# Gate logits gathered by expert in one PSUM bank, and no GpSimd in the last region of a fused attention and two-MoE kernel

## The chip, the cores and the metric

The kernel runs on one core of a Trainium2 chip. The metric is device time in microseconds of one execution of the whole program. The core has TensorE (matmuls; its weight loads are shown apart, as PEld), VectorE (DVE), ScalarE (ACT), GpSimd (POOL) and SyncE (SP), which here issues all loads and stores. [...]

## The reference, cut to what matters

```python
def reference(**kw):
    x = attn(**kw)                        # (4, 8, 768, 48) -> 3072 tokens x 384
    x = soft_moe(x, phi, w1, w2)          # 8 experts x 4 slots
    return top1_moe(x, w_gate, w1, w2)    # 8 experts

def attn(q, k, v, a_re, a_im):            # per batch and head, state S complex, 48 x 48
    for t in range(768):
        S = a[t][:, None] * S + outer(k[t], v[t])     # a scaled so that |a| <= 0.999
        y[t] = q[t] @ S.real

def soft_moe(x, phi, w1, w2):
    logits = x @ phi                                  # 3072 x 32
    d = softmax(logits, axis=0)
    slot_in = (d.T @ x).reshape(8, 4, 384)
    slot_out = concat(relu(slot_in[e] @ w1[e]) @ w2[e] for e in range(8))   # 32 x 384
    return softmax(logits, axis=1) @ slot_out

def top1_moe(x, w_gate, w1, w2):
    logits = x @ w_gate                               # 3072 x 8
    p = softmax(logits, axis=1)
    e = argmax(logits, axis=1)
    return p[e] * (relu(x @ w1[e]) @ w2[e])           # token by token
```

All arrays are 32-bit floats. w1 is 8 x 384 x 1024 and w2 is 8 x 1024 x 384, in each of the two MoE layers.

## The kernel before, in words

The 3072 tokens are 24 units `u` of 128 tokens (4 batches of 6 chunks). The program has three regions, and in each the work is first declared and then issued by a planner.

**Region 1** is the attention in chunks, the phi logits and the column softmax with its running sums. Its matmuls are small (48 to 128 rows and columns). Products of q, k and v with decay factors (the tiles F, line 573) are made on VectorE or GpSimd, and a part of F is copied by DMA into another layout (M, line 578). The first loads of soft-MoE weights ("late weight pieces", line 425) run here as soon as their buffers come free.

**Region 2** (lines 866 to 1117, declared in part by `decl_row`, `decl_dev` and `decl_c4`) is the soft-MoE: w1 and w2 of all eight experts over the 32 slots (L918, L947, L982), which gives the slot outputs so4 (L988). Beside it run the row softmax of all tokens, and its weights cc, which are split into high and low halves in c4. Since the softmax weights are close to uniform, the index `ei` of the second MoE's expert is found early, from the mean slot output, and the loads of that expert's weights (m1, m2) use it as a register.

**Region 3** (lines 1122 to 1307) is the second MoE. The transposes of L1054 turn c4 into cS, [96 features, 3072 tokens], copied out of PSUM six times (512 columns each). The gate weights for the slots, so4 times w_gate, are made at L1079 and split into W2S. The gate logits are 24 matmuls, one per unit: 128 tokens of cS against the 8 columns of W2S (L1089), all into one bank; the gate chain follows on VectorE (max, equality, exp, sum, reciprocal).

The two layers of the chosen expert are not computed token by token, since all tokens lie near the mean slot output. For 1024 hidden units, Gs = so4 times m1 (L1173, two halves of 512), is turned (L1180: G) and squared (ACT, L1177; L1181), and each hidden unit is sorted into "on for all tokens" (`pos`, L1184 to L1188), "off for all" or "mixed" (`mixed`, L1187), of which at most 96 are handled. The running counts of the mixed ones (L1193 to L1197) give `pf` (L1200), from which the selection matrix Pm is made by comparing with iota (L1202, two instructions, one per half). `Gp` (L1206) is G masked with `pos`; `PmF` (L1210, L1211) is the plain-float copy for the last two of the eight weight blocks. `Gl` (L1201) is G's low half. m2 is split into m2h (L1143) and m2l (L1145), in three pieces of two blocks. Then W, the matrix by which all tokens are multiplied, is summed in one PSUM bank `kb_a` by L1225 (plain), L1233, L1237 (m2h) and L1241 (m2l), and copied out as W0 (ACT, L1251) and W1 (DVE, L1252). The output stage has six groups of 512 tokens: one 512-column matmul for the hidden values (L1260), their relu and its low half (ACT or DVE L1261/L1262, DVE L1264), then for each of four units three 384-column matmuls (L1270, L1271, L1274), a copy out scaled by the gate (L1282 or L1283, ACT or DVE) and a store (SP).

**What sets the order.** An operation is declared with an engine, a modelled duration, what it reads and writes, and the other engines that could do it. `follow` (line 211) reads a string, ORDER[k], one 16-bit number per operation: operation number times four plus which alternative of engine. The order of the numbers is the order of issue, so every engine's queue follows from the string. `place` (line 148) then simulates it to hand out PSUM banks, and `emit` (line 223) issues it; where TensorE would be idle in that simulation, `emit` puts in dummy matmuls (line 844). The trace shows none of these in region 3. [...]

After the last region the program checks on the device that the shortcut held and branches to a full computation otherwise (line 1478 is in it); it is not taken here.

Of the kernel before, what the change touches and what calls it, by code (L numbers as in the profile page):

```python
# [44 lines left out]
def feature_rows():  # L45
# [24 lines left out]
    "8~`W)3;-Yi7yv8)6aX{;H~=sJ1OPn%KmY&$Q~<O9xBw6UXaHmY2mmAiL;y$tYyeCEyZ}%DZ~(yor~#A!bpV(EcmTx!kN}(jqyTvWYyofq<^Z4otN^e8d;ov|0Rqebr~p6#i~z_0)Bw={kO5o(_yFtx"  # L70
    "eFBsLm;s#ugaAYV$N`7|NCEu;p#h`;bOB5OtN{T5^#IHP`~Xn_@BnxL&;hUkd;wGev;l+xfC1b9xB*xJ)B))L7y;M--2sUKTmiuW!~y661OW&E3;`4Y*#YDM-~hY<904o=XaP6_5CQB0AOSoB-~sIc"
    "i~;EZ@Bw84U;$(Sa0BoHBmpP^Gy!M=fCBUa90CLa2m%cPFah}j6ax?f90M5wAOk=H`~oln6as_-C<9aji2_6eBm*o1FarPs1Or$DNdt5PGy?Pi_yLRpl>(3g7y}>zBmyV`m;#&vTmz{CGy@0&cmr$#"
    "Z~~wL5Cbd%OapWROaeFpJOV%hr2~8egac#)Py(z1r~+vN#01C$fCJzHqyh{BFb0eRECxgZv;w#SU;}Ielmom1hy#%Wm;=B9%mhUQNCH^`!~&cHumaEmL<L9%RRZt?Oa;&cNdzDT)dCO&6$Q8hyaUw)"
    "7zI!S*aRE}tOGO#wFCGB`~+MA!2<vV$O6m)umfQNPzA&T$O8xkOaxc}%mdT|&;!5(+yvkR4FymGp#vxdECo0QYy><8*aO@H3<LxPFa<aTGzH`Ycm(VO-~;3X=mYEnR0Z?{=mdNO_ybe~fCPvH@B@4X"
    "JOy0@U<9-Vbp!zfgam*FSp+}^lmwUr`~%nmTm@tWSOsAPga(`hpaf(DX$0f~R0g>P5D0Jti3ULhL<YPCqy&rvkOYkexCZnDaRo>QyavDq6bRG>-38bMumm^(Bn21<v;<%V;01UE=>>cRJppJ1WCo}N"
    "tOVr+Yz2S?hy_>%Yz7<%APATS#06*uU<gbG1O#;k#0G=~WC(Bu5CohCkOrg%j0I2zkOg!Flm!U{$Oh~M@CCpH$pxSWXb5Zw&<1!0^aWf7m<1FB%m%atC<dqo7zEt{BnYhroCTx>00smG*ap=G_yx=b"
    "6b6_Gkq2=IL<sx^@CKj-I0QHdJOmsBxCHbDoCu8v{00OE0SEa8d<ZB6ECjp>C<w3yv<J8e(FLdn90#BX2nM|blm@T`AO|c6Km-g1u?MUNy$9_E5C%vH=>|9lqzJeNJP1$-9R@H2Ob9RtR0!Y(Gz3`)"
    "p$7;D3<ul>7zX49bO<yEzy}Zq#0L}yzzHM=7zcm|hzL9fln12;m<PxQ&<7+0%m+{hTnh*YC<nv|+y~$X$O)_nAOu(ogb1hzkO(XXj0nsL<OeVZT?pt0)CaT(ya?<EKnU0eun4&b;0ZYiGzUQk_y=GM"
    "{RcP-MF#{5)CiOa-3Z_a><K&y<p@*>Kni3F@CVokJqhUu3<zKe00<lk2ns|B@CoDz_zBPns0#!L^a-2?XbaQ{Yzqtutqa5m00{&MSPAq8{0UtNR0rq@APVdVzzFaN^avCRC<<^3X$g1;BnkiuWC?T&"
    "fCp>|a0v(r5DGvEFbc>BL<w{W%?S7iGzlCDAPM{k*a^@GEDC%Hv<XNGObSp6+zAW`5D7F2Q3-$vhzX1d6bTp!SO;7OU<Y^!O$i7Mgb7s&kO?FSC<&AaWCvIZ<qDVyNCyNBO$TTPgbN@BNeLwej0<22"  # L80
    "=n8NLunV*cga@1nTncmti3fNK><Xv_pb4l6;0vt<kPDOx3=0(txC^BT<O^mB01M~~p$qH_5DN$km<yZ>#0z{2X$ou#a0(a;bP9Y5cnS;+@Cu|01Pg!)919=|5DgR!$P2s+gbFAN%nR5H^a>;k+zZqT"
    "hzigP7z!*4^b7q8_zUq1`U?CD7!9Zj=njkukP74ulnMb1fD0@QhzlGI1Pm|>KnpYrI14-rNee{_cn81>Fb!-6R1KI4SPe7{g$!H`><$bJFb{kOI1LC4ED0G56bz&aC=4(O91LI$j13?Rs0=L(febMW"
    "B@AQ@a19_0j0~9!JPkw*kqwj$hzytwKn+L@@D5B3oD4_|l?<Q^XbnsZuneUPtO~6RGz>Tlv<&<VBn@N?R12I9G!LK+d<>`!JPbe#xC~GXL<|rNXbi9lybM$f&<t1%U;x+(zzp;b)C@QeTnu0gYz_Dh"
    "qz%Xn#SO#^*bFEQ+zj9h3=d2Y%nWo5cnxt3Yz)B-v<kQiQ4R16><q9C)D5i-+zNmVObfgUcn<syoC<sm$O_F0Q42f|P!NO-;0h2AC=O%~We%YV-3_=6<P59{u?ZLt$PFA1(G4IENDtTzX%3tav<*}c"
    "SP*~?Xb)@;eGZHchz-pRC=c`vi4KqqgbpkZ01x;L=?o+faSxyn5DwrC<PDGxm=0_XybW*;l@9z3=nd=*To3>b01faBoDQH41P=%gKo4{eq!6SIC=#p=Ob-MO6b=**s19Hd2o6vWcn^UOd=G>VT@Q2+"
    "bq=%+xDLDys1OVe7!E`aSP#Gs#11SHunuGp&<d>(bPRb6R1e(`co2~f9S(pH(GJuQ)eeXc$PU;Jgb;`jxDWsk*$<2ll@OQ^)C!Cc-45*!*$`k4%?<<*^bC9ukPyTQ^bh?H2@v@Yun?FJoDY=`tPk7}"
    ";12Q+pbw}Iq!0KE<PWe9yb$0J=@2Xq;13`WzzWb0Xb`jy3=p^vz!1$4Fb?bx^$^Gq5D*j)7!WiLBoO5g@DRKY5E1zh01?CxJPsfZB@X-$v=AH+=?^pztq~Lvun|ZOOb!_l!4K3AP!b#wAQ8n6B@uKI"
    "FcK&bI1bPdJP|Y!ED$gdKoMCEc@jhsd=do_I1o4zJP-^KffBS4Y!Gk|C=o0XND(j*I1yY9$PqjeU=Ga@g%Ye1u@ck~*b!I~ToN=9h!P4Bv=WdKOc78K+!47F;1O66T@ld{^btT3z!6{)Y!XxvxDk{R"
    "WD-CQa1xjjr4q#vpb|t9WD!Ub!4mip<PrQ4yb|aUNDyce>=9rQ#1a4!yb;I}bP;e7@DX?s=o0J_OcJ0GP!0qV2oekuL=K!1d=Z2Z92FcA5E392R1(+{XcTP}@Ddagj1p`UkP%c47!s)xNE96t2ovBE"
    "_!9IIf)i;IbQ5qBq!E4-KoFD>kP~nebrdKS3=>5VP!tgp7!y<!OcYoY$PZi;fDvdBgcCFqI1`Bzj1z4U)Di*{loKEmBooXJsSy<toD(z^1QVGPC=)CbcoTROP!l{8pcAAMFcUx%L=&hJtP}haR1?e+"  # L90
    "xD!Ydyc56^<Pu;Mh!K1gj1hnouoHz8OcRI{#1qgG+!DwW)e~G3v=i79m=VkqoDo<P<P+!<>=W=4_!AHmloX5<oD`rGkQ6u-nH2OBq!g?a&=ar}v=pcmAQBuDAQS);B@+A-1QfUwycA^=z!cmQ$P^?L"
    "C=|sMU=!37;1gsMEEF&l*c1p9Bo#Ci+!W*#6cjuZ3=}XG5EVca%oO+(I27O%@Dvyn6crd1(G=(u{S@>REEPl)>=XzU3>5$s1Qh",
    "FaU@E000aD5CIec7y%psKmY^)2mlNK5C9YaAORQvGypgNMF2<uJOE7q8~`8yBmgJ?EC7rEd;lZ?C;==1Fab0HI029VoB){sJOMxfZ~$}wO#x8>Q~`JZL;*+vl>l4;PynC+WC3geSplQ~U;tnNr~p*}"
    "SO9bZWdK|NXaH>htN^e8gaCj5X#unVxB$cey#T-f$N<a$@BsJ#`~Uy}&;Zl`*Z|}J2mu5E-2mVK=m2p6c>(MI^Z)",
    ")ByMb&;Z;3%m9!8@B+vHC;%(~*Z=?km;e|65C9|rlmHw6ECDb8^a3aWGyyOH6aY8@-~d1YL;*Aar~o(s<NyQ!=>SLptN;iAJOJ<j_yGL?3;-Yi00Ha(^Z-Br1OW^IL;ySiv;dp{xBwIZOaZX~2mwd{"
    "Q~_N95CI(lPyr+Wpa8@GhyhFhSOJUyPyl2BVF4HcAOXMtbOBTVTmWbRSO9zhgaLp6gaEt%hyaWLkO5!-WB_acXaH;hZ~>$NsR5J$tO29|cmaR`m;syt`~m<2=mG2j1Oo^I90DK$umQ*cpaHZ2yaBlZ"
    "zya_96aypz)B)K690SY&Fak9KC;|)uPy$r~!~xs^-~rJAEdme%SONqB2?FE+NCNx;^Z@_@gaY{iKmv#YI06^~JpvR0MFLC$TmoSNi~?i=xB{30Xaal!oC1&nl>)E=Yyxxwr~+{Uy#l}jZ~$}wcmkjT"
# [1468 lines left out]
```

## Time and profile before

| | |
|---|---|
| Median of 3 runs | 293.49 us (292.86 to 293.55) |
| Profiled execution: its own time | 295.17 us |
| Profiled execution: span | 293.4 us, mean granted TensorE clock 0.96 |
| Busy, share of the span | TensorE 259.0 us (88%), weight loads 215.1 (73%), VectorE 222.4 (76%), ACT 208.5 (71%), GpSimd 85.3 (29%) |
| Moved by DMA | 65.41 MB, mean 223 GB/s |
| Region 1 / 2 / 3 end at about | 217 / 249 / 293 us of the span |

The profile is one execution recorded on the chip. Times are microseconds from the start of its span; the execution's own time is longer than the span, by what lies around it, and the median of the runs is another set of executions. A row of the chain of waits is a step of the work that ended last, followed backwards: its start, its length, the engine, the tile and the line. "issue" in it is time in which the engine waited for nothing that the profile shows. A timeline row is one instruction, or several alike in sequence; [x <- y] behind it is how long its engine had been idle and what ended that. The timeline's durations of matmuls are modelled ends and overlap each other, so the chain's lengths are used for sums.

### The profile page before, as it was taken

The numbers are of one execution on the slowest core, as the hardware profiler recorded it, in microseconds if no ns is written. First come the engines' busy times: TensorE is split into PE (matmuls) and PEld (weight loads), VectorE is DVE, ScalarE is ACT, GpSimd is POOL, SyncE is SP. The second block draws the span as 40 slices with busy tenths as digits, with TensorE's granted clock in tenths as the row PEclk, the third lists the DMA queues.
The fourth block names the chain that finished last, engine by engine and source line by source line (L and its number), as shares of the span: only waits on it lengthen the run. The fifth ranks groups of instructions, "written<-read, shape, count | busy, mean of one in ns | idle before, by whom it ended". The sixth has DMA issues, their size and how long they took to land.

```text
span 293.4 us, 11835 instructions
## 1 busy us (share of the span) xinstructions
PE 259.0 (88%) x4959; PEld 215.1 (73%) x4959; DVE 222.4 (76%) x489; ACT 208.5 (71%) x448; POOL 85.3 (29%) x128
## 2 busy tenths in 40 slices
...
GB/s 215 271 172 113 171 240 259 326 256 284 255 228 292 242 193 256 255 177 266 269 190 223 256 133 275 209 211 192 269 349 280 373 127 234 200 1 0 261 305 91
DMA packets 31789, 65.41 MB, mean 223 GB/s; under 512 B 3584, under 2 KB 16256, under 8 KB 31728
## 3 DMA queue, kind: packets, MB, share of 16 engines
...
## 4 chain that ended last, share of the span: by engine, by line
PE 62%; DMA 11%; DVE 10%; ACT 8%; issue 4%; POOL 0%; SPq 0%; DVEq 0%; POOLq 0%; ACTq 0%
PE bank L627 9%; PE bank L518 9%; PE bank L683 8%; PE bank L668 7%; DMA wr<-w 5%; PE bank L649 4%; PE bank L604 3%; DMA M<-F 3%; PE bank L947 3%; PE bank L716 3%; DMA kqi<-kq 2%; ACT L847 2%; DVE F L573 2%; PE bank L918 2%; PE bank L1270 1%
## 5 line engine op out<-in xcount | busy, mean ns | idle before, releaser
L627 PE MATMUL bank<-F 48*64 48x128 f32 (+1 forms) x1152 | 39.8, 247 | 1.1 <-DVE kqi L527 1.1
L627 PEld LDWEIGHTS bank<-F 48*64 48x64 f32 x1152 | 36.1, 133 | 3.7 <-DVE kqi L527 1.3
L847 ACT ACT_TABLE_LOAD x29 | 37.2, 1283 | 1.2 <-PEq L1549 0.8
L683 PE MATMUL bank<-sc,v 128*64 128x64 f32 x768 | 33.2, 234 | 1.8 <-POOL v L588 1.6
L683 PEld LDWEIGHTS bank<-sc,v 128*64 128x64 f32 x768 | 27.7, 145 | 7.5 <-issue 4.2
L668 PE MATMUL bank<-F,St 48*64 48x128 f32 x480 | 27.2, 278 | 4.3 <-issue 3.4
L518 PE MATMUL bank<-cst,wl 128*128 128x128 f32 x192 | 26.8, 281 | 2.4 <-ACT wl L490 2.4
L637 DVE TENSOR_TENSOR sc<-bank,cst 128x384 f32<-128x384 f32 x48 | 25.4, 549 | 3.5 <-PE bank L627 3.4
L518 PEld LDWEIGHTS bank<-cst,wl 128*128 128x128 f32 x192 | 23.5, 191 | 4.0 <-ACT wl L490 2.8
L668 PEld LDWEIGHTS bank<-F,St 48*64 48x64 f32 x480 | 18.8, 133 | 6.8 <-issue 4.9
L588 POOL COPY v<-v 64x192 f32<-64x192 f32 x31 | 14.0, 452 | 30.8 <-DVE F L573 11.1
L627 PE MATMUL bank<-M 48*64 48x64 f32 (+1 forms) x384 | 21.8, 245 | 1.2 <-DMA M<-F 1.2
L448 ACT COPY kT<-bank 128x96 f32<-128x96 f32 (+1 forms) x66 | 19.7, 355 | 4.2 <-PE bank L604 3.3
L649 PE MATMUL bank<-v,kT 128*48 128x48 f32 x640 | 21.4, 212 | 1.3 <-issue 1.3
L573 DVE TENSOR_TENSOR F<-kqi,wl 128x768 f32<-128x768 f32 x24 | 22.2, 957 | 0.4 <-ACT wl L553 0.2
L627 PEld LDWEIGHTS bank<-M 48*64 48x64 f32 x384 | 19.1, 134 | 2.3 <-DMA M<-F 1.4
L649 PEld LDWEIGHTS bank<-v,kT 128*48 128x48 f32 x640 | 17.9, 126 | 3.9 <-issue 2.9
L604 PE MATMUL bank<-cst,F 128*128 128x128 f32 x120 | 19.3, 284 | 0.2
L541 POOL TENSOR_TENSOR wl<-wl,n 128x384 f32<-128x384 f32 x12 | 12.1, 1006 | 23.9 <-DVE n L540 6.4
L448 ACT COPY yT<-bank 112x256 f32<-112x256 f32 x29 | 10.3, 374 | 12.0 <-PE bank L683 11.9
L573 POOL TENSOR_TENSOR F<-kqi,wl 128x768 f32<-128x768 f32 x8 | 14.7, 1833 | 11.3 <-PE bank L518 6.1
L668 PE MATMUL bank<-M,St 48*64 48x128 f32 x160 | 13.3, 286 | 2.3 <-issue 2.3
...
## 6 DMA issues: line engine op xcount, KB each, us to landing
...
v<-v SPq DMA_DIRECT2D x24, 288.0 KB, 4.2
...
```

The source lines that it names most:

```text
L448: v = {"A": ("ACT", t_act(n, True), lambda: nc.scalar.copy(out=out, in_=in_()), False), "D": ("DVE", t_dve(n), lambda: vec.tensor_copy(out ...
L518: pe.matmul(bank(kb)[:, 128 * i:128 * i + 128], lt[:, j, 128 * i:128 * i + 128], (tri, tri2)[j], start=True, stop=True)
L541: either("P", 384, lambda e: e.tensor_tensor(out=lt[:, 1], in0=lt[:, 1], in1=n, op=ALU.subtract), r=[kth, kn], w=[kth])
L573: either(e, 768, lambda e, i=i, b=b: e.tensor_tensor(out=Fv[:, i], in0=kq, in1=b, op=ALU.mult), r=[(kkq, 0), (kkq, 1), klt(u, i)], w=[kF[i]])
L588: alt=(("POOL", 350, lambda src=src, dst=dst: pool.tensor_copy(out=dst, in_=src), True), ("DVE", t_dve(192, True), lambda src=src, dst=dst ...
L604: pe.transpose(bank(kb)[:, 128 * j:128 * j + 128], F[:, j, 128 * x:128 * x + 128], idn)
L627: pe.matmul(o, kind(2 * m + y, i, x)[:, t:t + 64], kind(2 * m + y, i, 2 + x)[:, t:], start=(x == 0), stop=(x == 1))
L637: op("DVE", t_dve(384), lambda i=i, msk=msk: vec.tensor_tensor(out=sct[scs[i]], in0=bank(kbs[i])[:, :384].rearrange("p (m t) -> p m t", m= ...
L649: pe.matmul(kvps[64 * i:64 * i + 48, q, 48 * x:48 * x + 48], w, v[:, 48 * h:48 * h + 48], start=True, stop=True)
L668: pe.matmul(out(q, i, 64), S[64 * i:64 * i + 48, o:o + 64], kind(q, i, 2 + x), start=(x == 0), stop=False)
L683: pe.matmul(out(q, i, 64, 64 * b, 64), v[:, h:h + 64], sct[scs[i]][:, m, t:t + 64], start=(c == 0), stop=(c == 0 or b == 1))
L847: tab = lambda t: nc.scalar.preload_act_table_set(TABLES[t])
```

## The change

Four things change in the code; the cut diff shows them.

1. The column of the gate for unit u is `gx(u)` instead of u, in the scaling of the outputs and in the full computation.
2. W2S has 88 columns instead of 8. A new VectorE operation in region 2 fills them with zeros; the gate weights are written in columns 40 to 47. The logits are six matmuls, one per group of 512 tokens, with W2S as the weights (48 columns of it, in a window that moves by eight per group, so that group m's eight experts land in rows 8m to 8m + 7 of one bank) and 512 columns of cS moving. All six accumulate in the same bank. ACT (or VectorE) copies the [48, 512] result into `hid[0]`, and four transposes turn it into the bank from which the gate chain reads as before.
3. m2h, m2l and `Gp` lose their GpSimd alternative.
4. The three ORDER strings are new.

```diff
+def gx(u):
+    return 6 * (u % 4) + u // 4
...
-    W2S = t2("W2S", [128, NE], F32R)
+    W2S = t2("W2S", [128, 88], F32R)
+    V(88, lambda: vec.tensor_scalar(out=W2S, in0=tri[:, :88], scalar1=0.0, scalar2=None, op0=ALU.mult), [], ["W2Z"], True)
...
-        split(kb_g, W2S, NE, "W2S")
-        kb_l = s.bank()
+        split(kb_g, W2S[:, 40:48], NE, "W2S")
+        kb_t, kb_l, L = s.bank(), s.bank(), hid[0]
         for m in range(6):
-            def f(m=m):
-                for u in range(4 * m, 4 * m + 4):
-                    pe.matmul(bank(kb_l)[:, NE * u:NE * u + NE], cS[:96, 128 * u:128 * u + 128], W2S[:96], start=True, stop=True)
-            M(540, f, ["W2S", ("cS", m)] + ([kb_l] if m else []), [kb_l] + ([] if m else ["lg"]), None if m else kb_l)
+            M(250, lambda m=m: pe.matmul(bank(kb_t)[:48], W2S[:96, 40 - 8 * m:88 - 8 * m], cS[:96, 512 * m:512 * m + 512], start=(m == 0), stop=(m == 5)),
+              ["W2S", ("cS", m)] + ([kb_t] if m else []), [kb_t], None if m else kb_t)
+        AD("A", 512, lambda: nc.scalar.copy(out=L[:48], in_=bank(kb_t)[:48]), lambda: vec.tensor_copy(out=L[:48], in_=bank(kb_t)[:48]), [kb_t], ["lgT"])
+        def f():
+            for b in range(4):
+                pe.transpose(bank(kb_l)[:, 48 * b:48 * b + 48], L[:48, 128 * b:128 * b + 128], idn[:48, :48])
+        M(400, f, ["lgT"], [kb_l, "lg"], kb_l)
...
-           alt=(("DVE", ... m2h ...), ("POOL", ... m2h ...)))
-        either("D" if k % 2 else "P", n, ... m2l ...)
+           alt=(("DVE", ... m2h ...),))
+        either("D", n, both=False, ... m2l ...)
...
-        either("D", 64 * ns, ... Gp ...)
+        either("D", 64 * ns, both=False, ... Gp ...)
...
-            g1 = gate[:, u:u + 1]
+            g1 = gate[:, gx(u):gx(u) + 1]
```

What the new strings hold, decoded:

- Region 1 (1359 operations, the same ones): TensorE has 368 and SP 165 operations before and after; VectorE goes from 385 to 391, GpSimd from 114 to 109, ACT from 327 to 326; ACT table loads stay 29. Of the F products (L573) seven go from VectorE to GpSimd and four the other way. The load of w_gate goes from the 105th to the 121st of SP's operations. Of the late weight pieces, ten instead of five are issued ahead of unit 22's M copies (L578), and none instead of four after those of unit 23.
- Region 2: TensorE's order is the same. VectorE has the new zeros as its second operation, three of the six casts of c4 (one before) and one difference more than before. The six late loads of w2 change places among themselves.
- Region 3, GpSimd: three m2l and two Gp before, nothing after. All five go to VectorE.
- Region 3, VectorE after, from so4 on: small constants and zeros, cS of group 0, hc0 pf0 G0 mixed0, m2h piece 0, pf0 hc1 pf1 mixed1, Gl0 Pm0 Gl1 pos0 pos1 Gp0 pf1 Gp1 Pm1, m2l0, GpF, m2l1, m2l2, then the gate chain, W1 and the copies of the output stage.
- Region 3, TensorE after: gate weights, cS 5 0 1, Gs0, logits 0, cS2, sq0 G0, Gs1, cS4, counts 0, G1 sq1, cS3, logits 1, the zeroing of kb_a, logits 2, counts 1, logits 3, Gm0, logits 4, hi1, logits 5, lo0 hi2 Gm1 lo1, the four transposes, h0, ml1 A3 ml2 lo2 ml0 hi0 A4, then the output stage. (Gm is L1215; h0 the first L1260; lo and hi are L1233 and L1237, ml L1241, A L1225.) Before: cS 5 0 3 2, Gs1, gate weights, sq1 G1, the zeroing, Gs0, cS1, logits 0, G0, cS4, and so on.
- Region 3, SP: m1 in halves 0, 1 (before 1, 0), m2 in pieces 0 1 2 3 4 (before 1 2 0 4 3). The last store is 384 KB (before 192 KB). Of the 24 scaled copies of the outputs ACT has 14 and VectorE 10 (before 17 and 7).

## Rows read from the trace of the kernel before

**Rows 1.** Busy time by stretch: us, engines (instructions), granted clock, DMA share, GB/s.

```profile
core 0: us, PE busy (x) PEld busy (x) DVE busy (x) ACT busy (x) POOL busy (x), PEclk, DMA share, GB/s
230.00:240.00 10.00, 9.44 (x95) 3.74 (x94) 2.11 (x5) 3.70 (x10) 1.75 (x4) 1.00 0.77 268
...
256.00:257.00 1.00, 1.00 (x19) 1.00 (x18) 0.54 (x5) 0.83 (x2) 0.44 (x2) 1.00 0.00 0
257.00:264.00 7.00, 5.10 (x27) 4.97 (x26) 6.64 (x12) 0.36 (x1) 4.39 (x3) 0.55 0.00 1
...
271.00:282.00 11.00, 11.00 (x62) 10.40 (x62) 6.71 (x14) 9.10 (x17) 0.00 (x0) 1.00 0.72 267
```

**Rows 2.** The chain of waits: start, length, what.

```profile
135.73 2.28 issue
...
193.92 3.84 DMA M<-F
...
225.78 13.40 DMA wr<-w
...
248.06 0.57 DVE so L988
...
253.65 1.49 DVE pos L1188
...
258.07 1.66 DVE PmF L1210
259.73 2.09 DVE Pm L1202
...
268.25 0.35 PE bank L1241 x2
...
268.94 0.65 PE bank L1225 x2
```

**Rows 3.** Timelines of GpSimd, VectorE, TensorE and ACT, 251 to 262 us.

```profile
253.31 1.81 POOL L1145 TENSOR_TENSOR m2l<-wl,m2h 128x768 fp32r<-128x768 f32 x1 [20.49 <-PE bank L1173]
...
257.49 3.90 POOL L1145 TENSOR_TENSOR m2l<-wl,m2h 128x768 fp32r<-128x768 f32 x2
...
256.06 0.15 DVE L1188 SCALAR_TENSOR_TENSOR pos<-pos,mixed 128x4 f32<-128x4 f32 x1
...
257.13 0.81 DVE L1202 TENSOR_TENSOR Pm<-cst,pf 128x384 fp32r<-128x384 f32 x1
...
261.86 0.87 PE L1215 MATMUL bank<-Pm,G 128*96 128x96 f32 x4 [1.90 <-DVE Pm L1202]
...
251.04 0.28 ACT L1177 ACTIVATE sq<-bank 128x128 f32<-128x128 f32 x1 [0.68 <-PE bank L1173]
```

**Rows 4.** Groups of VectorE instructions by line and shape: busy, mean ns.

```profile
L573 DVE TENSOR_TENSOR F<-kqi,wl 128x768 f32<-128x768 f32 x24 | 22.2, 957 | 0.4 <-ACT wl L553 0.2 <-PE bank L668 0.2
...
L541 DVE TENSOR_TENSOR wl<-wl,n 128x384 f32<-128x384 f32 x4 | 2.2, 550 | 0.0
L1262 DVE TENSOR_SCALAR hh<-bank 128x512 fp32r<-128x512 f32 x3 | 2.1, 692 | 3.7 <-PE bank L1260 3.7
```

**Rows 5.** The chain of waits again, for TensorE's groups.

```profile
248.67 1.51 PE bank L1054 x12
...
250.19 0.79 PE bank L1173 x24
...
250.98 0.77 PE bank L1079 x6
...
251.96 0.33 PE bank L1180 x2
...
256.24 0.45 PE bank L1089 x4
...
274.45 0.23 PE bank L1260
```

**Rows 6.** Timeline of SyncE's queue, 200 to 222 us.

```profile
203.62 16.80 SPq L425 DMA_DIRECT2D wl<-w  x28
```

**Rows 7.** Waits: engine, line, waited for; us in total, times, longest.

```profile
PEld bank L683 <- issue: 4.2, 22, 0.4
```

More of the change, by code (lines that the diff above doesn't have):

```diff
@@ L69 @@
 ORDER = [
[L70 to L97, printed above, removed]
@@ new lines @@
+    ";1S>w<Pqo*1QA^kBo$>5OcGQQz!JR@C>3oI*%4q71{25<@DltH020I!>=ASkp%L&A&=QCe*b-0<R1WwNloEIm1QG}m3=*6Ym=dKD5EASX2oq2ga1tC6q!Dlt92KAvj1m|Uyb&N3sS>CWL=Jorgb@rA"
+    "5ff+;Y!ht}6cZg2X%pNM6cQN|0uyKyNEB@p$PdjAa1?YDgcFbxKoCR_fDw=pG!s-5SQLE|I1`x@loNpy_!5*6AQM~^oD<9v^b-9Nc@%sUP!s49BoinTJQHvebQ5_KR1+){pc60?j1hnoh!dm}OcX2?"
+    "I2EiDKodk0xD!Ydyc5(CmJ~1*h!Ln0U=)lKg%pSsuoL7GOcS&d%oETPz!St1G!@7b)f1QzoDo<PToc$6<P+!<Wfbfa@Dq#__!IOKoD{GWkQAU4q!gJHv=kr`tP}tg92BS&xD>n;z!W7C5ER4|AQZ?H"
+    "+!NswBortVEEF&lG!!@#U=w8%)D#312o(Gi*c3bz+!W*#6cj)d3=|O+%oO+(859&1;1uu_L=^oL7!}bJ>=XzU^b`yg02SyI1Qh",
@@ new lines @@
+    "hyVZpFaQhz5CIec1ONyC7y%psKmZ^CGypgN3;-knMF2<u5C9YaC;=D%8~`8yECDb9GyyySI01|RJOMxfL;+0zkN}wgQ2`_XC;%(~Spif5NCA`pOaWX0U;$|XZ2^1$PynC+qyU@%U;wB9Z~=7zcmaI@"
+    "Z~#>RfB<*^SO8@JTmWbQZ2)utumFSrv;epO!~nejzyQbq%mAza@BsJ#`~Uy}1OW&E&;Zl`WdYa#<N)0O-~i|V>;Uut",
+    "`~m<2_yU*!&;T$1<NzoD007hgGyn(yoB%igEC37upa9$e-~iYF>;Uut1px2>JOB^?qyYQ?_y80D009UAECDb9umB(c1p&MO3<0SCGyx<46ag3kH~~NbJOM}nOaUAL7yv*3=m10jL;+L*AORczTmeV`"
+    "C;?0W5CO;lPyr+Xv;c?!Pyko~zyNpwWC36SlmT!7tN>I1gaK>;bOE>kSO91N!~k3XWB_0QtO2kAi~+O(hyZ8+i~x`T%m8cvbO4+Im;sOhfB}2~paG--1Oo^IZ~*WDBm$@b^Z^V55Ca?oxB<igyaAK|"
@@ L99 @@
+    "!2!?#_yNcP)B)T9%>mc}<N+uGECT2O3<3}W6aoYS-~sFb`~esO2m&Ai00JBWi~^7XKmtetL;{ooOad?hGy+rtI0C=|m;yZlodQq-paP@<xB^%LTmq;9umZFK#RA9z)B@N7+ydbOtOCpecmQAmd;k;!"
+    "yaHqbXadm!@B-ul=>lv5a02WCBm?vUfB=L5d;)+1bOLz-gaU{H7y}>!C<6",
 ]
@@ L1143, in build @@
         op("ACT", t_act(n), lambda h=h: nc.scalar.copy(out=m2h[:, h], in_=m2[:, h]), r=[("m2", k)], w=[("m2h", k)], tab="E",
-           alt=(("DVE", t_dve(n, True), lambda h=h: vec.tensor_copy(out=m2h[:, h], in_=m2[:, h]), True), ("POOL", t_pool(n), lambda h=h: pool.tensor_copy(out=m2h[:, h], in_=m2[:, h]), True)))
-        either("D" if k % 2 else "P", n, lambda e, h=h: e.tensor_tensor(out=m2l[:, h], in0=m2[:, h], in1=m2h[:, h].bitcast(F32), op=ALU.subtract), r=[("m2", k), ("m2h", k)], w=[("m2l", k)])
+           alt=(("DVE", t_dve(n, True), lambda h=h: vec.tensor_copy(out=m2h[:, h], in_=m2[:, h]), True),))
+        either("D", n, both=False, fn=lambda e, h=h: e.tensor_tensor(out=m2l[:, h], in0=m2[:, h], in1=m2h[:, h].bitcast(F32), op=ALU.subtract), r=[("m2", k), ("m2h", k)], w=[("m2l", k)])
     Gs, sq = ([tf(f"{n}{i}", [128, 128]) for i in range(2)] for n in ("Gs", "sq"))
```

24 lines of the change are left out of this document (21 added, 3 removed).

## The prediction

> **What bounds it now.** The busy shares in the table are means over three regions with different limits, so I read the busy time by stage first. From 230 to 240 us TensorE (9.44 of 10 us) and the DMA engines (77%) are both nearly full. From 257 to 264 no bytes move, TensorE is busy for 5.10 of 7 us at a granted clock of 0.55, and VectorE (6.64) and GpSimd (4.39) are what is full. From 271 on TensorE runs without a gap at 1.00 [rows 1]. So the third region splits in two: the making of W (so4 ready at 248.06 + 0.57 = 248.63, the last accumulating matmul done at 268.94 + 0.65 = 269.59), and the output stage, a train of matmuls.
>
> The chain of waits tells what the 21 us of the first half are. It leaves TensorE three times for VectorE: `pos` L1188 for 1.49, `PmF` L1210 for 1.66, the second `Pm` L1202 for 2.09 us [rows 2]. These are not the lengths of that work: the same L1188 on the other half took 0.15, the first `Pm` 0.81. Beside the long ones stands GpSimd: one `m2l` from 253.31 to 255.12, just where the long L1188 ends, and two from 257.49 to 261.39, 0.4 us before the second `Pm` gets done [rows 3]. I read this as GpSimd stretching VectorE. [...]
>
> **Third region, removed.** GpSimd's five instructions go, and the stretching with them. L1188: 1.49 - 0.15 = 1.34 us. An L1202 without a neighbour isn't shown; the nearest row is a two-source 128x384 product from SBUF, 0.55 (L541), so the two lose 0.26 and 1.54. L1210's 192 elements lie between 0.15 (4 elements) and 0.55; I take 0.25, a loss of 1.41. Together 4.6 us, all on the chain [rows 2 to 4].
>
> **Added to VectorE.** Three `m2l` of 768 elements at 0.957 (L573, same shape), 2.9 us; `Gp` of 256 and 128 elements, 0.45 and 0.35 (bounds 0.15 and 0.55); one `m2h` cast (768 elements, one source; between 0.55 and 0.957, I take the lower end), one `cS` copy of 512 columns from PSUM, 0.69 (L1262) [rows 3, 4]. 4.9 us, nearly what the stretching cost: the gain isn't less VectorE time but where it lies. The `m2l` stand last in the new VectorE order, behind both `Pm`, and TensorE needs `Pm` first.
>
> **TensorE.** Out go 24 logits matmuls, 0.45 per four at full clock, 2.7 us. In come six of 512 columns, each as L1260 at full clock, 0.23; one 512-column copy on ACT (taken as VectorE's 0.69); four transposes, 0.50 (L1054, twelve in 1.51) [rows 4, 5]. The logits' way to the gate grows by copy and transposes; adding their VectorE chain behind the `m2l`, I get the gate half a us after the first output bank fills, and the seven banks cover that.
>
> **The sum along the new orders**, from 248.63 in the profiled execution [rows 2 to 5]. TensorE: gate weights 0.77, three groups of transposes 1.5, first half of Gs 0.79: 251.7. ACT's square and copy at 0.28: 252.3. Two small products at 0.33 (L1180) with Gs's second half, 0.79: 253.7. ACT again, one group of transposes and L1180: G's second half at 254.9. The loads are there: no bytes move after 256 [rows 1]. VectorE from 254.9: small ones 0.15 each (seven, 1.1), two `Gl` at 0.28 (half of L541's), two `Pm` 1.1, two `Gp` 0.8, and hand-overs of some 0.02: both `Pm` stand at 258.7, where before it was 259.73 + 2.09 = 261.82. Three `m2l` and `GpF` follow, 3.1: 261.8. TensorE works off meanwhile what has its operands; behind the last `m2l` stand four pairs of matmuls at 0.35 and one at 0.65, 2.05 [rows 2], so W is summed at 263.8 instead of 269.59: 5.8 us earlier. W's copies and the output train stay; its copies are shared 14 to 10 between ACT and VectorE (17 to 7 before) and the last store is 384 KB instead of 192 KB: I allow +0.3. The third region gives -5.5 us.
>
> **Second region.** W2S's zeros are one more VectorE instruction of 88 columns (0.15 to 0.55, I take 0.2) ahead of a softmax that the third region needs much later: nothing, under the wait of 13.40 us for weights that the chain shows until 239.18; without that cover 0.2 [rows 2]. Of the `c4` work one difference and two casts more fall to VectorE, under the same wait: nothing. TensorE's order is the same; the late loads change places, but the set that the first bf16 pass needs is whole one load before the last, and the last lands when it did.
>
> **First region.** The ACT table loads stay 29 and no instruction is added. Seven F products leave VectorE for GpSimd and four come back: VectorE -3 x 0.957 [rows 4], which small copies that change sides undo. The gate weights move from 105th to 121st of SP's 165 issues, 12 KB, first used at the end of the second region: nothing. The late weight pieces move too: ten instead of five stand ahead of the M copies of the last step but one, and none instead of four behind that point. A piece holds SP for 0.60 when its queue is full (28 in 16.80) [rows 6]. So those copies, whose landing is on the chain for 3.84, may come 5 x 0.60 = 3.0 us later, and what follows may end 4 x 0.60 = 2.4 earlier, though TensorE's 9.44 of 10 leaves only 0.5 of that. TensorE's stops in which it waited for nothing shown, 2.28 us at 135.73, may move or vanish with any new order [rows 1, 2]. I take nothing, and keep -2.5 and +3.0 for the range.
>
> [...] The weight loads of L683, 64 columns among matmuls of 48 to 128 rows, stood still 22 times with nothing shown to wait for: 4.2 us, 0.19 each [rows 7]. The new logits matmuls have 48 output rows among ones of 128. If each stops TensorE twice for as long, that is 6 x 2 x 0.19 = 2.3 us, from nothing, where no stop falls on the path, to this; no row has 48 columns beside 128 here. [...] Since TensorE has slack while VectorE makes `m2l`, I add nothing, and give it a case of its own below.
>
> **Rivals.**
> *Likeliest, 0.57.* As summed: -5.5 us. The profiled execution took 295.17 around a span of 293.4 and is 1.68 above the median of 293.49; nothing above hangs on that excess, so I subtract from the median: 288.0. Its own range, from the allowances of the sum, is 286.5 to 289.5.
>
> *The clock falls as before, 0.15.* For: it fell in this stretch. Against: the tiny logits matmuls and the 1.90 us wait are gone. If what is left at time t runs at half speed, W is done at t + 2 x (263.8 - t) = 527.6 - t; with the old t = 257 it is 270.6, and where waits absorb half of the doubling 267.2. Times 291 to 294.5.
>
> *The clock falls early, 0.07: slower.* By the same formula the new kernel loses from t = 258.0 down if nothing absorbs it; at 254.0 (TensorE waits there for ACT's copies) W is done at 273.6, +4.0: 297.5. For it: with the gate weights first, the transposes no longer run ahead of so4. Against it: 1.00 in the us before 257 in an order with as many waits [rows 1].
>
> *M copies queue behind weights, 0.11.* +3.0 on the forecast: 291.0. *Drains, 0.05*: +2.3, 290.3. *A vanished stop and the earlier weights tell, 0.05*: -2.5, 285.5.
>
> That GpSimd stays in the region is excluded: the new order holds none of it.
>
> **Numbers.** 0.3% is 0.9 us, about what a measurement can tell from no change here. Faster: 0.57 + 0.11 + 0.05 + 0.05 and 0.05 of the falling clock, 0.83; within: 0.05 of it; slower: 0.07 and its last 0.05, where first-region losses come on top, 0.12. The range reaches from the 285.0 of the case without a stop to 293.5, where the clock's fall eats nearly all.
>
> **What would show it.** Right: no GpSimd row after the second region; L1188 at 0.15, both L1202 near 0.55; granted clock 1.00 from 250 to the end of the outputs; W's first copy some 15 us after so4 (21 before). Wrong: a clock near 0.5 before W, VectorE ending `m2l` more than 13.5 us after so4, or an end of the first region that moves by more than 2 us.

## The result and the profile after

The changed kernel took 286.0 us (median of 4 runs, 283.95 to 286.47) beside 293.52 us for the kernel before in the same runs: ratio 0.973, 95% interval 0.967 to 0.978. In a later comparison on another occasion (e5 below) it was 288.3 us against 291.7, ratio 0.987 (0.977 to 0.996). The two intervals meet near 0.978, 6.5 us.

One thing is needed to read all that follows: executions differ here by some us before so4 is ready (it came at 246.0 and 247.6 us in the two traces of the changed kernel, and at 243.3 to 251.1 us in all fourteen, with no tie to the kernel that I can see). So I compare kernels by two stretches of the trace, which repeat better: from so4 to the first copy of W, and from there to the end of the span. Medians are of all executions, ratios leave disturbed ones out, so the two can differ by a per cent; the stretches decide then.

The stage view of the changed kernel (columns as in [rows 1]; PEclk is TensorE's granted clock as a share, at most 1.00 in every row):

```profile
core 0: us, PE busy (x) PEld busy (x) DVE busy (x) ACT busy (x) POOL busy (x), PEclk, DMA share, GB/s
230.00:240.00 10.00, 8.88 (x99) 4.03 (x99) 2.06 (x7) 2.46 (x6) 0.05 (x1) 1.00 0.50 175
254.43:261.43 7.00, 6.98 (x48) 5.59 (x47) 6.93 (x21) 3.94 (x8) 0.00 (x0) 1.00 0.00 1
257.00:264.00 7.00, 7.00 (x39) 5.28 (x38) 6.59 (x20) 2.87 (x7) 0.00 (x0) 1.00 0.00 0
```

Where before, from 257 to 264, TensorE worked 5.10 of 7 us at a clock of 0.55 beside a GpSimd busy for 4.39, it now works all 7 at 1.00 and GpSimd is silent; VectorE is as full as it was (6.59, before 6.64). Here W is summed at 262, so the last 2 us of that row are output stage. The row from 254.43 lies as far behind so4 as the row of before: TensorE 6.98 of 7 at 1.00. The chain of the changed kernel, from so4 on:

```profile
245.47 0.57 DVE so L993
...
246.08 0.83 PE bank L1086 x6
246.91 2.24 PE bank L1061 x12
249.15 1.44 PE bank L1184 x24
...
254.25 0.23 PE bank L1094
...
258.14 0.37 PE bank L1100 x4
...
260.64 0.35 PE bank L1252 x2
...
261.34 0.65 PE bank L1236 x2
...
277.60 0.58 ACT osb L1293
```

After so4 the chain stays on TensorE to the last output copy: none of VectorE's long steps of [rows 2] is left. TensorE's waits from 246 to 262 us are one line, and that one is for so4 itself:

```profile
PE bank L1086 <- DVE so L993: 0.6, 1, 0.6
```

so4 stands at 245.47 + 0.57 = 246.04, W is summed at 261.34 + 0.65 = 261.99: 16.0 us, where before it was 21.0. But two steps are longer than before: twelve transposes 2.24 (1.51 in [rows 5]), half of Gs 1.44 (0.79). The clock says why:

```profile
247.04:251.04 4.00, 4.00 (x39) 3.06 (x37) 1.88 (x6) 1.62 (x5) 0.00 (x0) 0.57 0.97 338
```

It fell about 1.2 us after so4 and was back 3.4 us later. VectorE's instructions, by line and shape (columns as in [rows 4]):

```profile
L1156 DVE TENSOR_TENSOR m2l<-wl,m2h 128x768 fp32r<-128x768 f32 x3 | 2.8, 947 | 0.0
...
L1213 DVE TENSOR_TENSOR Pm<-cst,pf 128x384 fp32r<-128x384 f32 x2 | 1.1, 548 | 0.0
...
L1155 DVE CAST m2h<-wl 128x768 fp32r<-128x768 f32 x1 | 0.5, 549 | 0.0
...
L1217 DVE TENSOR_TENSOR Pm<-G,pos 128x256 fp32r<-128x256 f32 x1 | 0.4, 424 | 0.0
L1217 DVE TENSOR_TENSOR Pm<-G,pos 128x128 fp32r<-128x128 f32 x1 | 0.3, 281 | 0.0
L1199 DVE SCALAR_TENSOR_TENSOR pos<-pos,mixed 128x4 f32<-128x4 f32 x2 | 0.2, 151 | 0.0
```

Both Pm take 0.55 (before 0.81 and 2.09 on the chain), both pos 0.15 (one was 1.49). The copy PmF (1.66 on the chain of before) stands on ACT now.

Between the two profiled executions, 293.4 - 284.7 = 8.7 us went: 2.6 before so4, 5.0 in the making of W, 1.1 from W to the end. The last lies behind the last output copy. The chain of before ended so:

```profile
284.11 1.15 DVE osb L1283 x2
...
285.71 0.07 DVE osb L1283
```

From W to the end of the last output copy it is 285.71 + 0.07 - 269.59 = 16.19 us there, and 277.60 + 0.58 - 261.99 = 16.19 now: the same, though before the last three copies stood on VectorE. What differs is SyncE's last two stores, before and after:

```profile
285.28 0.37 SPq L1285 DMA_DIRECT2D out<-osb  x1
285.80 1.53 SPq L1285 DMA_DIRECT2D out<-osb  x1
```

```profile
276.63 0.37 SPq L1296 DMA_DIRECT2D out<-osb  x1
278.21 0.37 SPq L1296 DMA_DIRECT2D out<-osb  x1
```

Before, the last store was issued 0.5 us behind the one ahead of it and held SyncE for 1.53 us; now it is 1.6 us behind and holds it for 0.37. The span ends 6.1 us behind that in both. From the end of the last output copy to the end of the span it is 7.2 to 7.6 us in the seven traces with the old order of region 3, and 6.4 to 6.7 in the seven with the new one. Why that issue takes longer no run shows.

### The profile page after: what moved, and what is told of

It reads as the page before. It is cut to its first block, busy times and chain, and to the rows that moved or that the text cites. A ratio compares the mean times of both kernels' runs of the same rounds, so it can differ in the third digit from the quotient of the medians.

```text
span 284.7 us, 11794 instructions
## 1 busy us (share of the span) xinstructions
PE 255.2 (90%) x4941; PEld 209.2 (73%) x4941; DVE 218.4 (77%) x504; ACT 207.9 (73%) x440; POOL 77.3 (27%) x117
## 4 chain that ended last, share of the span: by engine, by line
PE 53%; DMA 18%; DVE 14%; ACT 8%; issue 4%; SPq 1%; POOL 0%; DVEq 0%; ACTq 0%; POOLq 0%
PE bank L523 7%; PE bank L688 7%; DMA wr<-w 6%; PE bank L673 6%; PE bank L632 5%; DMA M<-F 4%; DMA kqi<-kq 4%; PE bank L654 3%; PE bank L952 3%; PE bank L923 2%; PE bank L609 2%; DVE F L578 2%; PE bank L721 2%; PE bank L1281 2%; DVE sc L642 2%
## 5 line engine op out<-in xcount | busy, mean ns | idle before, releaser
L688 PE MATMUL bank<-sc,v 128*64 128x64 f32 x768 | 32.2, 227 | 5.1 <-DVE sc L642 3.8
L688 PEld LDWEIGHTS bank<-sc,v 128*64 128x64 f32 x768 | 26.6, 138 | 10.5 <-issue 9.1
L523 PE MATMUL bank<-cst,wl 128*128 128x128 f32 x192 | 27.6, 287 | 0.3 <-ACT wl L495 0.3
L523 PEld LDWEIGHTS bank<-cst,wl 128*128 128x128 f32 x192 | 24.7, 200 | 1.6 <-issue 0.6
L578 POOL TENSOR_TENSOR F<-kqi,wl 128x768 f32<-128x768 f32 x10 | 18.3, 1833 | 16.6 <-PE bank L688 4.1
L654 PE MATMUL bank<-v,kT 128*48 128x48 f32 x640 | 20.5, 210 | 1.6 <-issue 1.6
L453 ACT COPY kT<-bank 128x96 f32<-128x96 f32 (+1 forms) x61 | 18.4, 346 | 4.5 <-PE bank L609 2.5
L578 DVE TENSOR_TENSOR F<-kqi,wl 128x768 f32<-128x768 f32 x22 | 20.3, 952 | 1.4 <-ACT wl L557 1.0
L712 POOL TENSOR_TENSOR St<-St,Dt 112x384 f32<-112x384 f32 x14 | 11.6, 830 | 13.9 <-DVE St L710 4.2
L532 DVE TENSOR_TENSOR kqi<-bank,kqi 128x384 f32<-128x384 f32 x24 | 13.1, 548 | 2.9 <-DMA kqi<-kq 2.7
## 6 DMA issues: line engine op xcount, KB each, us to landing
v<-v SPq DMA_DIRECT2D x24, 288.0 KB, 4.5
```

The source lines that it names most:

```text
L453: v = {"A": ("ACT", t_act(n, True), lambda: nc.scalar.copy(out=out, in_=in_()), False), "D": ("DVE", t_dve(n), lambda: vec.tensor_copy(out ...
L523: pe.matmul(bank(kb)[:, 128 * i:128 * i + 128], lt[:, j, 128 * i:128 * i + 128], (tri, tri2)[j], start=True, stop=True)
L532: op("DVE", t_dve(384), lambda: vec.tensor_tensor(out=kq[:, 0], in0=bank(kE0)[:, :384], in1=kq[:, 0], op=ALU.mult), r=[kE0, kkq], w=[(kkq, ...
L578: either(e, 768, lambda e, i=i, b=b: e.tensor_tensor(out=Fv[:, i], in0=kq, in1=b, op=ALU.mult), r=[(kkq, 0), (kkq, 1), klt(u, i)], w=[kF[i]])
L654: pe.matmul(kvps[64 * i:64 * i + 48, q, 48 * x:48 * x + 48], w, v[:, 48 * h:48 * h + 48], start=True, stop=True)
L688: pe.matmul(out(q, i, 64, 64 * b, 64), v[:, h:h + 64], sct[scs[i]][:, m, t:t + 64], start=(c == 0), stop=(c == 0 or b == 1))
```

## The experiments

All are compared by the stretches named above. so4 is the end of the row DVE so, W the start of ACT's copy of W.

| kernel | logits | GpSimd in region 3 | order of region 3 | so4 to W, us | W to end, us | clock below 1, from so4 to the last matmul |
|---|---|---|---|---|---|---|
| before | 24 small | in | old | 21.0 | 23.8 | from 9 us |
| e2 (region 1 new) | 24 small | in | old | 20.6 | 23.4 | from 8 us |
| e3 / e9 | 24 small | out | old | 23.2 / 20.9 | 23.5 / 23.5 | from 8 us |
| e11 | six | in | old | 21.2 | 23.5 | from 12 us |
| e12 | six | out | old | 19.4 | 23.5 | never |
| e7 | 24 small | out | new | 15.3 | 22.8 | never |
| e4 / e10 | six | back in | new, m2l moved | 20.6 / 23.4 | 22.6 / 22.8 | never / from 1 and from 15 us |
| after, e1, e5 | six | out | new | 16.0, 14.7, 14.7 | 22.7, 22.7, 22.8 | after only, from 1 us |
| e6 | six | out | new, transposes first | 15.0 | 22.7 | never |
| e8 | 24 small | in | old, gate weights first | 23.6 | 23.6 | from 1 and from 11 us |

### e1 and e2: the order of the first region

Two kernels, each with one string exchanged:

```diff
-ORDER[0] of the changed kernel      # e1: changed kernel
+ORDER[0] of the kernel before
-ORDER[0] of the kernel before       # e2: kernel before
+ORDER[0] of the changed kernel
```

> The changed kernel with the first region's order string of before; the rest as changed. Theory A (the gain comes from the making of W: 5.0 us of it between so4 and the end of W's sum, 1.1 in the output stage): about 287 us, ratio 0.978, so4 near 248 to 249 us and W summed 16 us after it. Theory B (the new order of the first region gives the half of the gain that the trace shows there, siT 4.1 us and so4 2.6 us earlier): 288.6 us or more, ratio 0.983 or more.

> The kernel before with the first region's order string of the changed kernel; nothing else. Theory A: 292.5 to 293.5 us (ratio 0.997 to 1.00), since what the profile of before has over its median (1.7 us) lies in its first region and is no cost of the order. Theory B: 290.5 to 291 us (ratio 0.990), so4 near 246 us.

e1: 285.5 us, ratio 0.973 (0.968 to 0.978), the very ratio of the changed kernel. e2: 293.8 us against 293.9, ratio 0.993 (0.985 to 1.001). e2's interval holds the ratio of either theory; e1's holds theory A's alone, so theory A holds: the first region's new order gives no gain beyond the spread, and the 2.6 us before so4 in the pair of profiles are no part of the change. (siT, on which the second region starts, came at 212.9 in e1 with the old order, and at 212.5 in e2 with the new one; in the profile of before at 217.0. so4 came at 244.5 and 244.0.)

### e3 and e9: GpSimd out alone

```diff
-alt=(("DVE", ... m2h ...), ("POOL", ... m2h ...))
+alt=(("DVE", ... m2h ...),)
-either("D" if k % 2 else "P", n, ... m2l ...)
+either("D", n, both=False, ... m2l ...)
-either("D", 64 * ns, ... Gp ...)
+either("D", 64 * ns, both=False, ... Gp ...)
-    s.emit(tab, fill(7), 300, 100)      # e9 only
+    s.emit(tab)                         # e9 only
```

> The kernel before with the GpSimd alternative of m2h, m2l and Gp removed and its order strings kept, so that the five operations stand in VectorE's queue where they stood in the order. Theory A (GpSimd stretched VectorE by 4.6 us, and the clock fell because of the wait for the stretched Pm): L1188 0.15 and L1202 0.55, clock 1.00 throughout, W summed about 17 to 18 us after so4, about 290 us (ratio 0.988). Rival C (the clock falls because of the tiny logits matmuls and counts, whatever VectorE does): the stretch is gone but the clock is 0.5 from about 257, W summed 19 to 20 us after so4, 292 us or more. Rival D (the long VectorE instructions are long for another reason): they stay long.

e3 took 294.6 us, ratio 0.999 (0.992 to 1.007): no gain at all. Only rival C had so little, and not W as late as 23.2 us after so4. One reason for that was in none of the cases. The planner, whose model now saw gaps on TensorE, had put in dummy matmuls, which really ran (TensorE's groups of 244 to 272 us):

```profile
L845 PE MATMUL bank<-cst 128*48 128x128 f32 x28 | 4.3, 318 | 0.0
```

So I took the dummies out as well:

> As e3 (GpSimd out of the third region, old logits, old order), but the planner puts no dummy matmuls into the third region: in e3 it had put in 28 of them, 4.2 us on the chain. Theory A' (e3 lost its gain to the dummies alone): clock 1.00, W summed 17 to 18 us after so4. Theory C' (with the old order TensorE's clock falls some 8 us after so4 with or without the stretching, and this takes the gain): VectorE done with both Pm about 10.5 us after so4 as in e3, clock 0.5 from 8 to 18 us, W summed 19 to 20.5 us after so4; time 290 to 293 us.

e9: 293.1 us against 293.8 (ratio 1.015, 1.006 to 1.025), W 20.9 us after so4. Its VectorE rows and the 6 us from 8 us after so4:

```profile
258.89 0.16 DVE L1188 SCALAR_TENSOR_TENSOR pos<-pos,mixed 128x4 f32<-128x4 f32 x1
...
260.87 0.55 DVE L1202 TENSOR_TENSOR Pm<-cst,pf 128x384 fp32r<-128x384 f32 x1
```

```profile
259.06:265.06 6.00, 5.60 (x26) 5.50 (x26) 4.21 (x14) 0.75 (x3) 0.00 (x0) 0.52 0.01 1
```

The stretching is gone, and both Pm are done at 261.4, 10.3 us after so4 (13.2 before). Yet the clock falls at the same place, and TensorE does the rest at 0.50 (each us from 260.06 to 269.06). Theory C' holds, though W came 0.4 us later than it said: in this order, with the small logits, the clock fell with VectorE late (before) and with VectorE on time (e9).

### e11 and e12: the new logits, alone and with GpSimd out, in the old order

```diff
 (kernel before)
-24 logits matmuls of 8 columns, u
+the zeros of W2S, six logits matmuls, copy, transposes, gx(u)
-ORDER[1], ORDER[2]
+the same with the new operations put in: zeros second in region 2; copy behind the last logits, transposes ahead of the gate chain
-    s.emit(tab, fill(7), 300, 100)
+    s.emit(tab)
```

e11 keeps the GpSimd alternatives, e12 doesn't.

> The kernel before with the new logits alone (six matmuls, copy, four transposes; zeros in the second region; gate columns by gx), GpSimd and the old order kept, no dummy matmuls. Theory C'' (the clock fell for the tiny logits matmuls among the waits): the stretching stays (L1188 1.5, PmF 1.7, Pm 2.1 us), clock 1.00 until the wait for Pm at the earliest, W summed 18 to 19.5 us after so4. Theory A (the wait and the order set the clock, not the logits): clock 0.5 from about 8 us after so4, W summed 20.5 to 22 us after so4.

> All of the change but the three new orders: new logits, no GpSimd, the old order strings with the three new operations put in, no dummy matmuls. If the order matters little: W summed 15 to 16 us after so4 as in the changed kernel, 286 to 288 us. If the order is what keeps TensorE fed and its clock up: clock 0.5 for part of the time, W summed 17 to 20 us after so4, 289 to 291 us.

e11: 292.9 us against 293.8 (1.016, 1.005 to 1.028), W after 21.2 us. Its VectorE timeline, and what TensorE waited for:

```profile
254.57 1.50 DVE L1199 SCALAR_TENSOR_TENSOR pos<-pos,mixed 128x4 f32<-128x4 f32 x1
...
260.57 2.15 DVE L1213 TENSOR_TENSOR Pm<-cst,pf 128x384 fp32r<-128x384 f32 x1
```

```profile
PE bank L1226 <- DVE Pm L1213: 3.0, 1, 3.0
```

The clock now stayed at 1.00 for 12 us after so4 instead of 8 to 9, so the small logits had a part in the earlier fall, as theory C'' says; but GpSimd's stretching kept Pm late, TensorE waited 3.0 us for it instead of 1.9, and the clock fell in that wait (0.97 in the us from 260.56, 0.50 in the next). Theory C'' was right on the clock and wrong on the time; the time is where theory A had it, for another reason.

e12: 293.6 us against 293.8 (1.005, 0.995 to 1.015), W after 19.4 us; the times show no gain, so what it gains, 1.6 us, rests on its trace alone. The clock is 1.00 all the way, and still TensorE works only 4.17 of 6 us:

```profile
251.36:257.36 6.00, 4.17 (x24) 2.76 (x24) 4.18 (x14) 1.24 (x4) 0.00 (x0) 1.00 0.00 0
...
257.36:263.36 6.00, 4.09 (x17) 2.48 (x17) 3.81 (x11) 0.48 (x1) 0.00 (x0) 1.00 0.00 0
```

```profile
PE bank L1252 <- DVE m2l L1156: 3.1, 2, 1.7
PE bank L1244 <- DVE Pm L1217: 0.8, 1, 0.8
```

In the old order two of the three m2l stand behind parts of the gate chain and of the output stage. GpSimd in the kernel before ended its last m2l 12.8 us after so4 (261.39 [rows 3]); on VectorE here the last two end 14.2 and 17.7 us after it, and TensorE waits 3.1 us for them. The second case of its expectation holds for W, by waits and not by the clock; the time that it gave, 289 to 291 us, was missed.

### e4 and e10: GpSimd given back

```diff
 (changed kernel, the three alternatives of e3 restored)
-ORDER[2]
+ORDER[2] with m2l 0, 1, 2 and Gp 0, 1 on GpSimd, each m2l right behind its m2h
-    s.emit(tab, fill(7), 300, 100)      # e10 only
+    s.emit(tab)                         # e10 only
```

> The changed kernel with three m2l (each right behind its m2h) and two Gp given back to GpSimd. Theory A: VectorE's instructions between 253 and 260 us grow two- to tenfold where GpSimd runs beside them, both Pm are done 2 to 4 us later, W is summed 18 to 20 us after so4, 288.5 to 290.5 us (ratio 0.983 to 0.990). Rival D: VectorE's durations stay (Pm 0.55) and, with 4 us of work taken from it, W is summed earlier: 285 us or less.

> As e4 (the changed kernel with five operations given back to GpSimd), but no dummy matmuls (e4 had 40, 5.0 us). If e4's loss of 6 us against the changed kernel was the dummies: W summed 15 to 16 us after so4. If it was GpSimd: its last instruction ends 14 us after so4 as in e4, behind it TensorE needs some 3 us, W summed 17 us after so4, 289 us; if TensorE's wait for it also brings the clock down, 18 to 20 us after so4.

e4: 294.3 us, ratio 1.000 (0.994 to 1.007), W after 20.6 us, later than theory A had it, with 40 dummies in it:

```profile
L850 PE MATMUL bank<-cst 128*48 128x128 f32 x40 | 5.0, 275 | 0.0
```

e10, without them: 295.8 us against 293.8 (1.025, 1.011 to 1.038), W after 23.4 us, later than any of its cases. So it is GpSimd, at least with its work queued in this order. Its timeline and VectorE's beside it, of e10:

```profile
255.28 1.83 POOL L1156 TENSOR_TENSOR m2l<-wl,m2h 128x768 fp32r<-128x768 f32 x1 [23.53 <-PE bank L1208]
258.52 0.61 POOL L1217 TENSOR_TENSOR Pm<-G,pos 128x256 fp32r<-128x256 f32 x1 [1.42 <-DVE pf L1211]
```

```profile
255.63 0.16 DVE L1195 COPY pos<-bank 128x4 f32<-128x4 f32 x1
255.82 1.29 DVE L1197 TENSOR_TENSOR pf<-pos 128x4 f32<-128x4 f32 x1
...
258.56 0.99 DVE L1213 TENSOR_TENSOR Pm<-cst,pf 128x384 fp32r<-128x384 f32 x1
```

The reader can see what kind of contention it is. A 4-column product from SBUF begins at 255.82 and ends at 257.11, with GpSimd's m2l (255.28 + 1.83). Pm begins at 258.56, GpSimd's Gp ends at 259.13, and Pm ends 0.42 after that, at 259.55. By these rows it doesn't run slowly; it stands until the other is done (alone it takes 0.55, so some 0.1 of it is not held up). The second Pm of before agrees: GpSimd ends at 261.39 and Pm 0.43 after it, at 261.82 [rows 3]. The copy from PSUM at 255.63 beside the same m2l takes 0.16, as in the changed kernel (253.69), where GpSimd has nothing. But the blocking is the smaller part: both Pm are done only 1.1 us later than in the changed kernel, at the same clock (e4 beside e5, 10.3 and 9.2 us after so4), where theory A said 2 to 4. TensorE waits for GpSimd itself, whose last instruction, a Gp behind all three m2l, ends 15 us after so4:

```profile
PE bank L1248 <- POOL Pm L1217: 3.3, 2, 3.0
```

In that wait the clock fell (1.00 until 261.96, 0.50 from 262.96 on). In e4, where dummies filled the wait, it stayed at 1.00, and W came earlier.

### e5 to e8: the clock at so4, and the logits in the new order

e5 is the changed kernel itself. The others:

```diff
-gate weights, cS 5, cS 0            # e6: changed kernel, TensorE's order
+cS 5, cS 0, gate weights
-six logits matmuls, copy, transposes, gx(u)     # e7: changed kernel
+24 logits matmuls of 8 columns, u
-cS 5, ... , sq1, gate weights       # e8: kernel before, TensorE's order
+gate weights, cS 5, ...
```

> The changed kernel itself, for comparison with the next three on one chip: about 286 us (ratio 0.974), W summed 16 us after so4, the clock at 0.5 from about 1 to 4.5 us after so4.

> The changed kernel with the first two groups of cS transposes (L1061) ahead of the gate weights (L1086) in TensorE's queue, so that it has work while so4 is made. Theory A (the clock fell at so4 because TensorE stood idle for 0.65 us there): clock 1.00 from so4 on, W summed 14.4 us after so4 instead of 15.9, 1.5 us less than the changed kernel, 284.5 us. Rival E (the clock falls for the tiny matmuls of the gate weights or for what came before so4): the same time as the changed kernel within 0.5 us.

> The changed kernel with the 24 logits matmuls of 8 columns instead of six of 48 rows, the copy and the four transposes; the orders otherwise kept. Theory A (the logits lie in TensorE's slack and don't set the clock): within 1 us of the changed kernel, clock 1.00 from 252 to the outputs. Rival C (the tiny logits matmuls make the clock fall): clock 0.5 in the making of W, W summed 18 to 20 us after so4, 288.5 us or more. Rival F (the new logits cost drains): 1 to 2 us faster than the changed kernel.

> The kernel before with its gate weights first in TensorE's queue of the third region, as the changed kernel has them. Theory A: TensorE idles while so4 is made, the clock falls to 0.5 about 1 us after so4 and is back some 3 us later, 1.5 us more on the chain: 295 us (ratio 1.005). Rival E: no fall there, 293 to 294 us.

e5: 288.3 us, and the clock did not fall at so4 (compare the row 247.04 of the first profile):

```profile
248.59:252.59 4.00, 3.81 (x65) 3.18 (x66) 2.31 (x9) 2.26 (x6) 0.00 (x0) 1.00 0.96 338
```

W came 14.7 us after so4 instead of 16.0. So the early fall belongs to one execution, not to the kernel, and cost 1.3 us here. e8 had it, too: 295.0 us, ratio 1.012 (1.005 to 1.018):

```profile
248.33:252.33 4.00, 4.00 (x41) 3.29 (x38) 0.75 (x5) 1.16 (x2) 0.00 (x0) 0.57 0.97 341
```

W came after 23.6 us there, 2.6 later than before; four dummies (0.6 us) have a part in that beside the fall.

Of the seven traces with the gate weights first (after, e1, e4, e5, e7, e8, e10) three had this fall; of the seven with transposes first, none. TensorE stands 0.6 to 0.7 us for so4 in the former and 0.2 in the latter. That fits theory A but is too few to settle it. e6, with transposes first, is not faster: 288.3 us, ratio 0.982 (0.973 to 0.992), W after 15.0 us, because it ran into the next wait, for a copy of cS:

```profile
PE bank L1094 <- DVE cS L453: 1.0, 1, 1.0
```

e7: 290.4 us, ratio 0.990 (0.985 to 0.996), W after 15.3 us against 14.7 in e5. In the new order the 24 small logits took 0.7 us more and left the clock at 1.00; theory A, and not rival F, by which they would have been faster. The weight loads of the six new matmuls stood still for 0.4 us in all with nothing shown to wait for (changed kernel, idle time last):

```profile
L1094 PEld LDWEIGHTS bank<-cS,W2S 96*48 96x48 f32 x6 | 0.8, 127 | 0.4 <-issue 0.4
```

No kernel of these beats the changed one by more than the spread.

## Why the prediction was right, and where it was not

**The time and its main term.** 288.0 was forecast with a range of 285.0 to 293.5; 286.0 and 288.3 were measured, the first 0.5 below the likeliest case's own range. The stretch from so4 to W was forecast to shrink by 5.8 us and shrank by 5.0 in the profiled pair, 6.3 from before to e5. VectorE's prices were right to 0.1 us: m2l 0.95 for 0.957, Gp 0.42 and 0.28 for 0.45 and 0.35, pos 0.15, Pm 0.55, and in e9 the unblocked L1210 takes the 0.25 that was guessed:

```profile
260.70 0.25 DVE L1210 COPY PmF<-Pm 128x192 f32<-128x192 f32 x1
```

**Where the sum was lucky.** It let VectorE's `m2l` set W: both Pm 10.1 us after so4, the m2l done at 13.2, 2.05 more to W, 15.2 in all. In the profile they came at 10.5, 13.2 and 16.0, but with 1.3 us of the clock's early fall in each. Without the fall (e5) it is 9.2, 11.9 and 14.7. So VectorE was 0.9 to 1.3 us earlier than summed: its instructions follow each other closer than their lengths (in the profile of the changed kernel a Gl of 0.28 us begins at 254.29 and the first Pm at 254.49), where the sum added hand-overs. The rest on TensorE took 2.8 us instead of 2.05. The two errors nearly cancel. The path was another: "TensorE has slack while VectorE makes `m2l`" is not so. Between so4 and W TensorE waits for nothing in the profile, for 0.2 us (a copy of cS) in e5, and is busy for 14.40 of 14.66 us there. What remains is TensorE's own work.

**What carries the gain.** The step "GpSimd's five instructions go, and the stretching with them ... 4.6 us, all on the chain" measured each piece rightly, but alone it is worth nothing (e9: 20.9 us against 21.0). The new logits alone are worth nothing either (e11: 21.2). Both together give 1.6 us (e12: 19.4), and the new order, which puts the m2l right behind Pm and ahead of the gate chain, gives the remaining 3.4 to 4.8 (after and e5). The strings of regions 2 and 3 were exchanged together, and TensorE's order with VectorE's, so which part of the order does it isn't shown. With the new order and GpSimd out, the new logits add only 0.7 (e7). One view of the stretch from so4 to W, of before, e9, e11, e12 and e5 in turn, shows why:

```profile
core 0: us, PE busy (x) PEld busy (x) DVE busy (x) ACT busy (x) POOL busy (x), PEclk, DMA share, GB/s
248.63:269.62 20.99, 18.57 (x152) 16.53 (x152) 14.22 (x41) 6.78 (x16) 6.65 (x5) 0.76 0.24 84
251.10:272.04 20.94, 19.39 (x152) 16.69 (x152) 12.79 (x46) 6.79 (x17) 0.00 (x0) 0.76 0.24 85
249.54:270.75 21.21, 17.32 (x138) 13.33 (x138) 14.51 (x41) 7.25 (x17) 6.65 (x5) 0.84 0.16 54
243.33:262.76 19.43, 15.31 (x138) 10.98 (x138) 12.74 (x46) 7.25 (x18) 0.00 (x0) 1.00 0.26 91
247.59:262.25 14.66, 14.40 (x142) 11.61 (x142) 12.12 (x43) 7.82 (x19) 0.00 (x0) 1.00 0.34 120
```

TensorE's idle time is 2.4, 1.6, 3.9, 4.1 and 0.3 us, and its clock 0.76, 0.76, 0.84, 1.00 and 1.00. In before a mean of 0.76 means half the clock for about 10 of 21 us, 1.9 of them idle; the estimate from these rows is that the fall cost (10 - 1.9) / 2, some 4 us, and the waits 2.4. GpSimd out alone leaves the fall. The new logits alone put it off, and the waits grow. Both together end the fall and leave 4.1 us of waits; with the new order they go too. The prediction said that the place of the m2l matters and summed along the new order, which is why the sum came out; it didn't say that the order is the largest term.

**The clock.** A fall because of the late Pm, theory A of e3, is refuted as the cause in the kernel before: the clock fell before that wait began ([rows 1] and [rows 3]: below 1.00 from some point after 257 on, the wait from 260.0), and it fell in e9 without the stretching. In before it was at 0.50 in each us from 258.63 to 267.63, the half speed that the formula of the prediction takes. In the old order it fell with the small logits and both Pm on time (e9, from 8 us after so4); with the new logits it fell in the wait for the late Pm (e11, from 12 us) and stayed at 1.00 without GpSimd (e12). In the new order the small logits left it at 1.00 (e7).

**The early fall.** The rival that had the clock fall early came half true: its reason, the gate weights ahead of the transposes, fits, but the fall came 1.2 us after so4 and not 5.4 (254.0), was over after 3.4 us and not at the end of W, and isn't there each time. Its price was 1.3 us, not 9.8.

**The signs of being wrong.** Two of the three that the prediction named stood in the profile: a clock near 0.5 before W, and a first region that ended 4.1 us earlier (siT). e5 and e1 show that neither belongs to the change; m2l ended at 13.2 us, inside its limit.

**Drains** were given 2.3 us and 0.05, by the stops of L683 [rows 7]. No run shows such stops at the new logits: their weight loads stood still for 0.4 us in all (L1094), and with the 24 small ones in their place W came 0.7 us later (e7 against e5). **The first region**: nothing was taken, and e1 and e2 show nothing. The case of the M copies didn't occur.

**The output stage** was the term of the wrong sign: +0.3 was allowed for the copies' new sharing and the larger last store; it gained 0.8 to 1.1. The sharing changed nothing up to the last copy (16.19 us in both profiles). The gain is SyncE's: the last store held it for 1.53 us and now for 0.37, a term that the sum didn't have. e12, with the old order and all else changed, has 7.35 us from the end of the last copy to the end of the span (7.62 before, 6.52 now) and 23.5 from W, so this too is the order's.
